# A hand-written order of instructions on TensorE, ScalarE and VectorE, re-ordered between a tenth and three eighths of the run

## The chip, the cores and the metric

The kernel runs on one core of one Trainium2 chip. The metric is the device time of one execution in microseconds (us). The profile gives beside it the span of one profiled execution and a row for every instruction. The engines are named as in the profile: PE is TensorE (matmuls), DVE is VectorE, ACT is ScalarE, POOL is GpSimd and SP is SyncE; the last two mostly issue DMAs here. A name such as L517 is line 517 of the kernel.

## The reference

Two stages. The first is an attention over a global and a local window, for 4 batches, 8 heads, 768 positions and 64 elements a head; the second is a feed-forward layer on the 3072 tokens that come out of it, with a squared relu between its two products.

```python
scores = scale * np.matmul(q, k.transpose(0, 1, 3, 2))
rel = pos[:, None] - pos[None, :]
is_global = pos[None, :] < 8
is_local = (rel >= 0) & (rel < 96)
scores = scores + bias                    # a slope per head times the distance
scores = np.where(is_global | is_local, scores, -1000000000.0)
a = softmax(scores);  attn_out = np.matmul(a, v)
x = attn_out.transpose(0, 2, 1, 3).reshape(3072, 512)
h = np.maximum(x @ w_in, 0.0)             # 512 to 2048
out = (h * h) @ w_out                     # 2048 to 512
```

## The kernel before, in words

**Tiling.** The 3072 tokens are cut into eight half-batches of 384 tokens, half 0 to half 7. Each goes through the same stages: its queries, keys and values are loaded by DMAs that GpSimd issues; queries and keys are turned (on TensorE for the first three halves, by DMA transposes that SP issues, `turn_by_dma`, from half 3 on); score jobs on TensorE (`score_unit`, L639, with 64 rows) fill two PSUM banks, ScalarE takes the exponential (L652), VectorE multiplies by a mask that holds the window and the slopes (`weigh`, L676); attention jobs multiply by the values (L700, or L1490 for the first two halves) and VectorE divides by the sums (`norm`: a reciprocal and a product, L708 and L710, or L1502 and L1504). The result is turned into `xt`, the transposed input of the feed-forward layer: by TensorE (`tile_to_x`, L1519) for halves 0 and 1, by SP's DMA transposes (L725) later.

**Layer 1.** For half 0, most of half 1 and a part of the others, plain jobs (`layer1`, L746) fill a PSUM bank with up to 512 columns; a relu on ScalarE (L773) or VectorE (L775) empties the bank, and a square on either (L787, L789) writes the hidden layer. The other groups of columns are computed with seven products in place of eight (L870), from weights that were added and subtracted beforehand (`in_mix`) and from sums of the tokens.

**Layer 2.** The first tile of tokens is plain (`layer2`, L1007). The others go in pairs of tiles with seven products (`layer2_pair`, L1093) from differences of quarters of w_out. These are made by `weight_sum` in `list_mix` (L517), in halves, c = 0 and c = 1. The first of these operations subtracts two parts of the same chunk of w_out, chunk c. w_out itself comes by four DMAs of a quarter each (`list_w_out`, L490), issued by GpSimd.

**What sets the order.** Every instruction group is an operation, listed once with what it needs. A string, `ORDER`, then says in which sequence they are emitted. A word has a letter for the engine (p TensorE, a ScalarE, d VectorE, g GpSimd, s SP, l a load on GpSimd's DMA queue) and a number: for p and l the number of the job in TensorE's or the loads' own list, for the others the number in one common list. So a124 and d124 are the same operation on two engines. Digits after a dot are the PSUM banks (0 to 7) that a TensorE job takes; a job without them goes on in a bank that it shares. An `@` names an SP operation that a load is to follow.

```python
for word in ORDER.split():
    ...
    op = lists.get(word[0], self.rest)[int(word[1:])]
    self.now, self.spare = [int(i) for i in banks], int(spare or 0) / 100
    op.result = op.emit("POOL" if word[0] == "l" else self.LETTERS[word[0]])
```

Each engine runs its own words strictly in their sequence and waits at a word whose data or whose buffer is not ready. The words of different engines do not order one another, except that data, PSUM banks and buffers pass in the order of emission. A job that takes a bank must wait until the operation that empties the bank's former holder is done.

Words that the prediction speaks of: d145 is the first half of the first weight difference (L517, c = 0), and l25 is the load of chunk 0 of w_out. d123 is the norm of attention job p55 (half 1). p49, p58 and p60 are plain layer-1 jobs of half 0, p56, p62, p63 and p65 of half 1, each over 512 columns of a bank (two groups of 128 hidden columns for 256 tokens, or four for 128 tokens). d131 is the relu of p60, d115 that of p49, and d122 and d129 are squares behind such relus. p72, p73, p74, p75 and p81 are plain layer-1 jobs of half 1 over 384 columns (one group for 384 tokens). p59 and p61 turn a piece of half 1's `xt` (L1519). p93 is an attention job of half 2, which needs the weighing d198. p106 and p107 are score jobs of half 3; p97, p100, p102, p104, p109 and p142 are products of layer 2 (L1093); p170 is an attention job of half 4. d221 is a norm of half 2, s222 the DMA transpose of its result, and s214 and s215 turn half 3's keys and queries.

Of the kernel before, what the change touches and what calls it, by code (L numbers as in the profile page):

```python
# [68 lines left out]
a138 d208 a209 d238 p91.5 a180 p92 d148 a142 s215 d217 p94.7 p102 d223 p95 d181 a243 d219 p96.2  # L69
d237 s218 p100.3 d236 p109 a216 d212 s224 d226 p104 d220 d241 l42 s227 d211 p107.57 d225 p108.23  # L70
d152 l41 p97 a253 s213 d256 a254 d139 l38@215 p99 a249 d143 d270 a250 l40@215 p111 a232 d188 l43
p112.23 d252 p106.57 p103.4 d190 a246 l39@215 a259 d244 p105 a260 l44 d251 d257 a247 p113.52
d255 s258 l45 p114.13 p116.0 s233 d228 a262 d248 p129.7 l46 a263 d230 p115.5 a266 d261 p120.2
a290 d229 p119.1 a271 d264 a267 d231 p123.7 d210 a269 d278 p122 s322 p125.3 d282 a281 p124 d239
a276 p121.5 d265 a291 p135.7 d283 s323 d279 a285 p117.6 a284 p130 a277 p127.1 d292 p128 p138
d321 a299 p140 a288 d268 p132.5 a305 a289 d272 s240 p126.7 a306 s280 p133 d286 p131.2 a308 p134
d296 p139.6 s273 d298 a297 l48@323 p141.7 a295 d307 p137 d324 s287 l54 d522 p136 a303 d393 p110
a301 l51 d309 a310 p118 d304 a300 l49@323 d293 p144.05 p145.63 d302 a328 l50 s294 p143.17 d311
a331 p142.2 d316 l47@323 a329 d317 a332 p146.0 l52 a274 d319 p147.6 a325 d431 l55 a320 a326
p149.53 d330 p148.41 l53 p150 d312 a336 d318 a337 d327 p157.7 a335 p155.4 a339 d334 p170.1 a350  # L80
d338 p151 a340 d368 a348 p158.0 a342 p167.5 s369 d313 p156.3 d351 p160 p159 d349 p152.1 a353
d314 p164.0 d395 a345 p162.3 s396 p161 d354 p154 d315 d356 p169.7 d357 a364 s397 p163 d341 p165
a358 p179.3 d360 a361 a359 d333 p168 p173 d343 a355 p175 d365 p172.4 d373 a376 p171.6 s245
p176.0 a381 d371 s275 s352 p174 d367 p178 d366 p153.3 a370 l56@397 d347 a377 s372 p166.4 d380
a374 a382 d398 l63 p177 p181 d378 a362 p180.7 l60 a346 p182 d383 a375 l57@397 p183.0 d379 s384
a387 a385 l61 a363 p186.14 d386 p185.63 p184.72 a403 p187.5 l71 d399 a407 a411 d400 l59 p188.6
a404 d414 d401 a408 l58@397 p189 a405 d394 a412 d410 p191.15 l62 d409 p192.73 a415 p190.24 a416
d413 p193 a420 d389 a417 p198.1 a418 d427 p204.2 a424 d435 p196.6 d390 p217.4 s436 d391 a432
d406 a425 p205.7 p202.1 d392 a445 s344 d487 p208 d441 a460 p200.3 a449 d426 a421 p197.4 d402
p209 a439 p211 d433 p195.1 p215.5 a430 d454 s434 p203.3 p216.4 d422 a442 d450 a443 p194 d478  # L90
s489 a459 d474 d458 p201.7 p213.2 d440 p221 s490 a456 p219 d423 a451 d419 p206 p207 d479 a446
p218 d481 a467 p220.4 d475 a444 p212 d465 p225.7 d429 s388 l68 p210.6 d455 s466 p199 d447 a462
l64 d491 a461 p214.4 d452 p222 a482 l67@490 p223 d457 a437 s453 a469 p228 d471 l70 d463 p224
s428 a494 d468 p229.36 l65@490 s488 a472 p234.04 d476 p231.15 a495 d470 p226.2 a501 l69 d480
d477 a496 p227.3 d492 l66@490 a507 d483 a502 d473 p239.1 l72 p233 a508 d503 a525 l73 d497
p235.62 a493 a464 p230.05 p232 d523 d484 a498 a448 p243.4 d504 p238.0 d506 s505 p245 a510 d513
p244.3 a531 p237 d486 a530 d485 a524 d514 p253 a499 p248 d518 p257.6 d542 s519 p247.5 d529
p241.7 p250 d534 a533 p236.4 d527 a538 d515 a511 s574 p251 a547 d500 p259.3 a517 p254 a549 d512
p255.7 s438 p268 d543 p261 d544 p242 a551 a563 d539 p246.2 a528 d509 p266.7 a532 p270 d559 a564
p265 p249.1 d558 p258.5 a540 s560 p260 d535 p267 d548 p256.7 a561 s545 p264 d546 a566 p240.5  # L100
a550 d536 s575 p252.6 d516 a526 p262 a576 p269 d552 p272 d565 d541 p263.0 p271 d577 p273 d567
a578 a553 d556 p277 d554 a562 d583 p279.1 s555 a594 a568 a557 p274.76 d569 p275.30 s537 p276.52
a584 p278 d598 a591 d599 a587 p280.7 d601 a602 a585 d596 p284 a592 d600 s597 a588 s572 p282.53
d586 p281.64 a603 p283.20 a607 d593 p287 a614 d666 a611 p289 a604 d617 d579 a605 d570 p286.5
a608 d620 s573 p288.2 d580 a618 p301.6 d589 s571 p304.4 d610 a637 p292 d606 a616 a641 d609
p321.3 a612 d669 d624 p303.0 p305 d640 p308 a642 p290.7 d582 d619 p293 a621 p319.0 d581 a626
d645 p294 d662 p310 a627 d613 p296 s663 p299 d648 p285.2 d630 p306.4 a615 s625 p295.0 d634 s595
p320 d643 p311.1 a664 p297.7 d590 a649 p312 d629 a646 p291.6 d650 p309.0 d622 p298 p314 a633
d647 p313 s623 a631 p316.6 d667 p300.0 a632 d670 p307 a665 d653 p318 p302 d651 a660 p324 d635
p322.1 d656 s636 a677 a661 d644 p323.5 d638 s657 d668 p315 a676 p317 a652 p333.0 d671 p341.6  # L110
p326 a705 a639 p332.7 d680 p325 a696 d675 d697 a654 p344.1 a658 d672 p347.4 a655 d710 p335.2
p349 a713 d699 p340 a659 p336.1 d681 p339.2 d678 a715 p353 d673 s679 a703 d700 p327.5 s628 d719
a704 d685 p338 d688 p357 d682 p346 d726 p343 p348.1 d712 a702 p337.4 d686 a714 p328 a701 a689
p345 d720 p352 p342 d708 p330 d674 a718 d706 a709 d683 p358 d711 p360 p329.2 d687 a731 d707 p355
d684 a692 p359 p351.4 a729 p364.6 d717 a690 a727 s691 d723 a693 p350.0 a728 d730 p331 a732 p356
d694 p354 d716 a695 p334 a724 d721 a725 d741 p363.3 d744 a722 p361 d745 d742 d698 p375.7 d737
# [1608 lines left out]
```

## Time and profile before

| | |
|---|---|
| median of three runs | 200.37 us (200.17 to 201.5) |
| the profiled execution's own time | 200.18 us |
| its span | 198.4 us |
| PE busy | 191.6 us, 2400 matmuls |
| DVE busy | 176.7 us, 448 instructions |
| ACT busy | 151.7 us, 321 instructions |
| POOL busy | 64.5 us, 80 instructions |
| granted TensorE clock | 1.0 |

The span runs from the first to the last instruction of the program in the profile; 1.8 us of the execution lie outside it. Busy time counts an engine's instructions and leaves waits out; PE's share of the span is therefore near one when it has few waits. Groups of the page have the line, the engine, what is written and read, the tile, the count, then busy time and mean, then the idle time ahead of them and what ended most of it. In the timeline a row has the start, the duration, the engine, the line and the operation; a bracket holds the idle time just before it and what ended it. In the chain of waits a row is a stretch of the chain that ended last.

### The profile page before, as it was taken

The numbers are of one execution on the slowest core, as the hardware profiler recorded it, in microseconds if no ns is written. First come the engines' busy times: TensorE is split into PE (matmuls) and PEld (weight loads), VectorE is DVE, ScalarE is ACT, GpSimd is POOL, SyncE is SP. The second block draws the span as 40 slices with busy tenths as digits, with TensorE's granted clock in tenths as the row PEclk, the third lists the DMA queues.
The fourth block names the chain that finished last, engine by engine and source line by source line (L and its number), as shares of the span: only waits on it lengthen the run. The fifth ranks groups of instructions, "written<-read, shape, count | busy, mean of one in ns | idle before, by whom it ended". The sixth has DMA issues, their size and how long they took to land.

```text
span 198.4 us, 6012 instructions
## 1 busy us (share of the span) xinstructions
PE 191.6 (97%) x2400; PEld 163.4 (82%) x2400; DVE 176.7 (89%) x448; ACT 151.7 (76%) x321; POOL 64.5 (32%) x80
## 2 busy tenths in 40 slices
PE   7998999999998999999999999999999999999993
PEld 3776899757997587789888998999889999999993
DVE  6778899899999989999989999899899996978971
ACT  6999997979444988966999679878897588769211
POOL 8985456637006902930392008600000000000000
DMA  5999999999997999999899599995531311201214
GB/s 154 189 185 201 194 171 180 207 184 155 175 182 73 178 181 227 114 132 133 228 128 151 93 218 134 167 182 128 96 101 37 115 36 40 107 2 56 106 53 159
DMA packets 102859, 27.52 MB, mean 139 GB/s; under 512 B 92976, under 2 KB 99888, under 8 KB 102832
## 3 DMA queue, kind: packets, MB, share of 16 engines
q0 software_dynamic: 70816, 13.11, 85.5%
q1 hardware_dynamic: 30816, 13.45, 30.1%
q10 hardware_dynamic: 1200, 0.59, 1.1%
q8 instruction: 18, 0.29, 0.6%
q14 instruction: 9, 0.07, 0.2%
HBM read 27.26 MB, written 6.29 MB: 169 GB/s over the span
## 4 chain that ended last, share of the span: by engine, by line
PE 69%; DMA 12%; DVE 9%; POOL 5%; issue 2%; SPq 1%; ACT 0%; POOLq 0%; DVEq 0%
PE yps L1093 27%; PE hps L870 19%; PE hps L746 13%; DMA v<-in_v_dram 7%; PE av L700 3%; DMA q<-sq 3%; PE sp L639 3%; DMA vb<-v 2%; PE yps L1007 2%; POOL sk L411 1%; POOL v L411 1%; POOL w_mix L422 1%; POOL sq L411 1%; DVE mixed L1058 1%; PE av L1490 1%
## 5 line engine op out<-in xcount | busy, mean ns | idle before, releaser
L652 ACT ACTIVATE ex<-sp 128x512 f16<-128x512 f32 x66 | 36.3, 632 | 5.7 <-PE sp L639 5.4
L1093 PEld LDWEIGHTS <-h 128*128 128x128 f16 x376 | 33.9, 98 | 4.3 <-DVE h L955 0.2
L746 PE MATMUL hps<-xt,w_in_sb 128*128 128x128 f16 (+2 forms) x288 | 35.7, 273 | 0.0
L255 ACT COPY kept<-hps 128x384 f32<-128x384 f32 x52 | 24.6, 490 | 12.2 <-PE hps L870 9.6
L930 DVE CUSTOM_DVE_ANT_0 hr<-hps,kept 128x384 f16<-128x384 f32 x58 | 30.4, 549 | 1.1 <-PE hps L870 0.6
L746 PEld LDWEIGHTS <-w_in_sb 128*128 128x128 f16 x288 | 23.5, 98 | 5.7
L1093 PEld LDWEIGHTS <-mixed 128*128 128x128 f16 x272 | 25.2, 98 | 3.6 <-DVE mixed L1058 0.2
L255 ACT COPY y<-yps 128x256 f32<-128x256 f32 (+2 forms) x39 | 14.8, 391 | 16.6 <-PE yps L1093 16.5
L411 POOL DMA_DIRECT2D sq<-in_q_dram x19 | 17.2, 906 | 31.3 <-DMA q<-sq 26.3
L411 POOL DMA_DIRECT2D sk<-in_k_dram x19 | 16.9, 893 | 26.1 <-DMA q<-sq 20.7
L870 PEld LDWEIGHTS <-w_in_sb 128*128 128x128 f16 x288 | 24.4, 98 | 0.9
L870 PEld LDWEIGHTS <-in_mix 128*128 128x128 f16 x272 | 22.8, 98 | 0.9
L870 PE MATMUL hps<-x_mix,in_mix 128*128 128x192 f16 x204 | 23.4, 246 | 0.0
L411 POOL DMA_DIRECT2D v<-in_v_dram x24 | 21.6, 911 | 2.9 <-DMA w_mix<-in_k_dram 1.5
L1093 PE MATMUL yps<-w_mix,h 128*128 128x256 f16 (+1 forms) x192 | 22.4, 264 | 0.0
L1093 PE MATMUL yps<-w_mix,mixed 128*128 128x256 f16 (+1 forms) x184 | 22.2, 268 | 0.0
L1093 PE MATMUL yps<-w_out_sb,h 128*128 128x256 f16 (+1 forms) x184 | 22.1, 268 | 0.1
L676 DVE TENSOR_TENSOR phat<-ex,mask 128x1024 f16<-128x1024 f16 (+1 forms) x36 | 20.7, 593 | 0.4 <-ACT ex L652 0.2
L953 ACT ACTIVATE h<-hr 128x768 f16<-128x768 f16 x25 | 20.9, 857 | 0.0
L870 PE MATMUL hps<-xt,w_in_sb 128*128 128x192 f16 x172 | 19.8, 246 | 0.0
L773 ACT ACTIVATE hr<-hps 128x384 f16<-128x384 f32 (+1 forms) x32 | 16.6, 555 | 0.8 <-PE hps L746 0.8
L787 ACT ACTIVATE h<-hr 128x768 f16<-128x768 f16 (+1 forms) x19 | 14.2, 771 | 1.1 <-DVE hr L775 1.1
(112 smaller groups left out, 353.3 us busy)
## 6 DMA issues: line engine op xcount, KB each, us to landing
out_dram<-y SPq DMA_DIRECT2D x23, 256.0 KB, 2.9
v<-in_v_dram POOLq DMA_DIRECT2D x24, 128.0 KB, 6.8
sq<-in_q_dram POOLq DMA_DIRECT2D x19, 128.0 KB, 6.2
sk<-in_k_dram POOLq DMA_DIRECT2D x19, 128.0 KB, 6.3
w_in_sb<-in_moe_w_in_dram POOLq DMA_DIRECT2D x4, 512.0 KB, 11.6
w_out_sb<-in_moe_w_out_dram POOLq DMA_DIRECT2D x4, 512.0 KB, 10.6
y<-in_k_dram ACTq DMA_DIRECT2D x2, 256.0 KB, 5.1
y<-in_q_dram SPq DMA_DIRECT2D x2, 256.0 KB, 4.5
```

What stands on the lines that cost most here:

```text
L255: nc.scalar.copy(out=out, in_=in_)
L411: dma = nc.gpsimd.dma_start(out=dst, in_=src[x.b, :, r0 + t * P:r0 + (t + 1) * P, :] .rearrange("h p d -> p h d"))
L639: nc.tensor.matmul(sp[h][:, i, :], lhsT=lhsT, rhs=queries(x, r % HT)[rows, a, :], start=True, stop=True)
L652: nc.scalar.activation(out=st["ex"][:, h], in_=sp[h], func=AF.Exp, scale=scale)
L676: eng(e).tensor_tensor(out=x.phat[a][:, :, t0:t0 + n], op=ALU.mult, in0=st["ex"][:, :, i0:i0 + 2 * n].rearrange("p e (t b) c -> p e t (b c ...
L746: nc.tensor.matmul(st["ps"][:, i * n:(i + 1) * n], lhsT=w_in_sb[:, kk, m * P:(m + 1) * P], rhs=x.xt[:, kk, c0:c1], start=kk == 0, stop=kk ...
L773: nc.scalar.activation(out=o, in_=i, func=AF.Relu)
L787: nc.scalar.activation(out=h2, in_=hr, func=AF.Square)
L870: nc.tensor.matmul(st[name][:, i * HC:(i + 1) * HC], lhsT=left(i, kk), rhs=right(kk), start=fresh and i == kk == 0, stop=kk == KK - 1, ski ...
L930: eng(e)._custom_dve(dve_ops.TENSOR_ADD_SAT, out=hidden(which)[:, :, cols], in0=sums(name), in1=st[kept], s0=3.4e38, s1=0.0)
L953: nc.scalar.activation(out=h2, in_=hr, func=AF.Square)
L1093: nc.tensor.matmul(st[bank_name][:, 0:n], lhsT=a(m), rhs=b(m)[:, cols], start=fresh and m == 0, stop=m == HK - 1, skip_group_check=not fresh)
```

## The change

Only the string `ORDER` differs. Each engine's operations are the same ones, and GpSimd's, SP's and the loads' words keep their sequence among themselves. The first part (to about 19 us, TensorE's first 35 jobs) keeps TensorE's sequence too. From there on 99 of TensorE's jobs, from p39 to about p136, stand at another place in its sequence; ScalarE's and VectorE's words are in another sequence as far as that, and 25 operations that VectorE did are done by ScalarE, 22 the other way round. From job p142 on the sequence of every engine is the old one. PSUM banks are dealt out anew all through the string. The core of the diff, the lines that hold the words named above:

```diff
--- before.py
+++ after.py
@@ -49,74 +49,74 @@
 KEEP = [0, 1, 2, 1, 6, 4, 3]
 
...
-d59 a61 p33.1 d67 p32.43 l17 a62 d83 p31.20 a23 p34.1 l21 p35.5 a79 d63 d84 a75 d89 l20 p39.4
-a76 d85 a80 l16 p38.12 a27 p37.05 p36.3 a99 l18 d64 a71 d81 p40.4 l25 a72 d87 a95 d82 p42.7 l26
-d73 p43.3 a90 d74 l27 a101 d105 p46.6 a91 d77 l28 d94 a96 p50.1 p45.0 l22 a100 p47.4 d78 d97
-a117 a86 d109 l23 p44.7 p41.5 a110 d108 p57.2 a102 d93 a112 d103 p48.1 p51.0 p49.6 a106 d88 d104
-a126 p53.7 p60.4 d98 a118 a115 d92 p55.5 a113 p52.3 d123 p54.2 a127 d111 a120 a114 d189 p61.0
-p58.6 a131 d119 p63.5 d121 p59.7 d203 p62.1 a122 d107 a130 d128 a133 p56.4 a134 d116 a129 d135
-p68.3 a132 p67.2 p70.7 a154 d199 p69.0 a157 d163 p81.6 d204 l32 a155 d124 p72.1 a164 a156 l24
-d165 p75.2 d160 a167 d158 a136 d161 p71.7 l29 d159 a172 d137 p87.41 a185 d205 p76.30 l33 p78.52
-d166 a173 p79.6 d187 a174 l31 p74.7 a196 d175 a179 p80.3 l30 d162 a197 d200 p82.0 d184 l34 d202
-p77.45 d145 l35 p86.13 p83 a193 d206 d147 a168 l36 p65.1 d182 a186 l37 d149 p84 a194 d150 a176
-p85 d198 a177 d125 p88.6 d146 a191 a183 d178 s192 p73.3 d153 a140 p89.4 a170 d141 a169 d201
-p93.5 a171 d207 p98.0 d195 p90 d234 d221 p101.1 d520 s222 d521 p64.7 a242 d235 d151 p66.3 s214
-a138 d208 a209 d238 p91.5 a180 p92 d148 a142 s215 d217 p94.7 p102 d223 p95 d181 a243 d219 p96.2
-d237 s218 p100.3 d236 p109 a216 d212 s224 d226 p104 d220 d241 l42 s227 d211 p107.57 d225 p108.23
...
+l21 p30.72 a61 d59 p33.1 d67 p32.43 a62 l20 d83 a23 p31.60 p34.5 a79 l16 d63 p35.1 a75 d84 d89
+l18 a27 p36.4 a80 d64 l25 a71 p39.5 d87 a76 l26 d82 p38.63 a72 p37.74 d94 l27 p40.0 a99 d81 l28
+a90 d88 p45.2 d85 a95 p46.5 l22 d73 a96 d109 p42.7 a110 l23 p57.1 d74 a91 d77 d105 p43.6 a100
+d78 a101 p41.3 d93 a111 p51.2 d97 p50.5 p44.4 d103 a86 p47.7 d104 a126 p53.0 p58.3 d117 d92 d108
+p54.1 a128 d98 d102 a118 p52.5 a106 p48.4 p60.3 d119 d120 d189 p59.2 p55.6 a130 p49.5 a112 d114
+d123 a127 p65.0 d145 a121 a113 p70.2 d131 p61.4 p69.7 d122 a133 p67.6 d129 p68.1 d115 a154 p75.3
+a163 l32 a132 p80.4 d164 d160 a157 l24 d107 p72.5 d155 a140 d149 p79.2 l29 a158 d187 a165 p81.6
+a182 l33 p71.0 a116 d203 d161 a172 l31 p82.1 d184 a185 d147 a162 l30 p56.2 a166 d199 d159 d156
+l34 p73.7 d167 a124 d141 p77.34 d169 l35 p86.60 a176 p87.52 d204 p83 a196 d146 l36 a177 d205
+p76.73 a193 d168 l37 p63.5 a183 d153 d200 p78.46 a197 p84 d151 a173 d178 a186 p88.2 d520 a179
+d198 p85 a194 d201 d206 p93.7 a191 p74.4 d221 a180 s192 p89.0 a207 d195 s222 a170 a174 d150
+p62.1 a136 d181 s214 p90 a171 d202 d175 a134 p94.7 p96.6 d212 s215 a208 d137 p91.4 a125 d211
+p66.3 d148 a135 d217 p92 a142 d223 a209 s218 p98.5 a216 d270 p64.1 d234 s224 d226 p95 d219 s227
+d152 p101.4 a220 a138 d225 d235 p97 l42 s213 a242 a238 d236 a143 p106.37 l41 p108.61 d188 p102
...
```

More of the change, by code (lines that the diff above doesn't have):

```diff
@@ L75 @@
[L75 to L92, printed above, removed]
@@ new lines @@
+d198 p85 a194 d201 d206 p93.7 a191 p74.4 d221 a180 s192 p89.0 a207 d195 s222 a170 a174 d150
+p62.1 a136 d181 s214 p90 a171 d202 d175 a134 p94.7 p96.6 d212 s215 a208 d137 p91.4 a125 d211
+p66.3 d148 a135 d217 p92 a142 d223 a209 s218 p98.5 a216 d270 p64.1 d234 s224 d226 p95 d219 s227
+d152 p101.4 a220 a138 d225 d235 p97 l42 s213 a242 a238 d236 a143 p106.37 l41 p108.61 d188 p102
+a253 l38@215 a246 d237 p99 a232 d243 l40@215 a247 d228 a254 p112.63 d248 p107.07 l43 a259 p104
+d230 a249 d229 l39@215 d231 a260 p120.1 d255 p116.6 a250 l44 d239 p109 a271 d244 a139 d190 l45
@@ new lines @@
+p113.03 p114.27 a262 p119.4 d261 l46 a278 d252 a266 p122 d276 p124 a267 p125.0 d256 p127.2 d521
+p129.4 d281 d210 p115.7 a290 d283 a285 p111 a263 d284 d268 p100.4 a288 a269 d264 a257 p130 d241
+s258 p133 d292 s233 p138 s322 p128 p123.3 d289 p121.7 d296 p140 s323 d282 a297 p134 d308 p126.5
+a291 p136 d277 p103.4 a305 d251 a309 s240 d298 p117.3 d265 a306 p139.6 d279 a324 p132.1 d272
+s280 p137 d286 a301 l48@323 p141.7 s273 d303 p105 l54 d522 a304 d321 p135.3 s287 l51 d393 p131.2
+a299 p110 l49@323 d293 a307 a295 p118 d302 a310 l50 s294 a300 d311 p144.50 l47@323 p145.36 a328
@@ new lines @@
+d316 p143.21 p142.7 a331 d317 l52 a329 d319 p146.5 a332 l55 d431 a274 p147.3 d330 l53 a325 a320
+d312 p149.06 a326 d318 p148.42 p150 a336 d327 a337 d334 p157.1 a335 d338 p155.4 a339 p170.5 a350
+p151 d368 a340 a348 p158.2 d313 s369 a342 p167.0 d351 p156.6 p160 d349 p159 s396 p152.5 d314
+a353 d395 p164.2 a345 p162.6 d354 p161 s397 p154 d315 d356 d357 p169.1 a364 p163 d341 p165 s245
+a358 d360 p179.6 s275 a361 s352 d333 a359 p168 p173 d343 a355 p175 d365 p172.4 d373 p171.3 a376
+p176.2 d371 a381 p174 d367 s372 p178 d366 p153.6 a370 l56@397 d347 a377 p166.4 d380 a374 a382
@@ new lines @@
+d398 l63 p177 p181 a362 d378 p180.1 l60 a346 p182 d383 a375 l57@397 p183.2 d379 s384 a387 a385
+l61 a363 p186.54 d386 p185.36 p184.17 a403 l71 p187.0 d399 a407 a411 d400 l59 p188.3 a404 d414
+d401 a408 l58@397 p189 a405 d394 a412 l62 p191.50 d410 p192.16 a415 d409 p190.74 a416 d413 p193
+a420 a417 d389 p198.5 a418 d427 a424 d435 p204.7 d390 p196.3 s436 d391 p217.4 d406 a432 a425
+p205.1 d392 s344 d487 p202.5 a445 p208 d441 a460 p200.6 a449 d426 a421 p197.4 d402 p209 a439
+p211 d433 p195.5 p215.0 a430 d454 p203.6 s434 p216.4 d422 a442 d450 a443 p194 d478 s489 a459
@@ new lines @@
+d474 d458 p201.1 p213.7 d440 p221 s490 a456 p219 d423 a451 p206 d419 p207 d479 a446 p218 d481
+a467 p220.4 s388 d475 a444 p212 d465 p225.1 d429 s466 p210.3 d455 p199 d447 a462 d491 a461
+p214.4 d452 p222 a482 l68 p223 d457 a437 s453 a469 p228 d471 l64 d463 p224 s428 a494 d468
+p229.63 a472 s488 l67@490 p234.24 d476 p231.50 a495 d470 p226.7 a501 l70 d480 d477 a496 p227.6
+d492 l65@490 a507 d483 a502 d473 p239.5 l69 p233 a508 d503 a525 d497 l66@490 p235.37 a493 a464
+p230.20 d523 p232 l72 d484 a498 a448 p243.4 d504 l73 p238.2 d506 s505 p245 a510 d513 p244.6 a531
@@ L122 @@
+a729 p364.3 d717 a690 a727 s691 d723 a693 p350.2 a728 d730 p331 a732 p356 d694 p354 d716 a695
+p334 a724 d721 a725 d741 p363.6 d744 a722 p361 d745 d742 d698 p375.1 d737 d733 p362 d738 s734
+d740 d739 p365.2 a735 d743 s736 p366 a747 d752 d756 d759 p369.5 d755 p371.4 a760 d748 p367 d753
+a763 d757 p372.7 d754 d767 d749 p374 d746 p373 d758 s750 p368 d766 a765 a764 p378 d751 p376 d771
+p377 d768 s772 p370 d769 s770 p379 a761 p380 s762 d773 s774 a775 a776"""
 class Op:
```

59 lines of the change are left out of this document (23 added, 36 removed).

## The prediction

> **What bounds the kernel now.** I read the page's busy times first, then a table of stretches around the part that is rewritten, then the places where TensorE really stands still, and last the landings of the loads. Page, busy time and DMA slices:
>
> ```profile
> PE 191.6 (97%) x2400; PEld 163.4 (82%) x2400; DVE 176.7 (89%) x448; ACT 151.7 (76%) x321; POOL 64.5 (32%) x80
> ...
> DMA  5999999999997999999899599995531311201214
> ```
>
> Busy time by stretches (per engine: us busy and instructions; last the mean DMA share times the stretch and GB/s):
>
> ```profile
> 18.00:36.00 18.00, 17.91 (x261) 16.23 (x259) 15.46 (x45) 16.70 (x37) 9.13 (x11) 1.00 1.76 185
> 36.00:52.00 16.00, 16.00 (x153) 10.71 (x150) 15.90 (x41) 12.90 (x27) 8.80 (x10) 1.00 1.87 183
> 52.00:60.00 8.00, 8.00 (x113) 7.41 (x110) 7.86 (x20) 4.16 (x8) 0.00 (x0) 1.00 1.23 160
> 60.00:75.00 15.00, 14.45 (x173) 10.79 (x171) 13.88 (x35) 11.80 (x26) 7.88 (x9) 1.00 1.57 149
> 75.00:87.00 12.00, 11.62 (x151) 8.83 (x149) 11.72 (x29) 10.75 (x24) 7.91 (x9) 1.00 1.61 161
> ```
>
> TensorE (third column of figures) is the bound: hardly a hole from 18 to 87. VectorE (fifth) has no slack from 36 to 60 (23.76 of 24 us), so nothing there can be late without being late for good. The DMA engines are nine tenths busy or more in every slice from 5 to 60 us. So a new order can win only the small holes of TensorE and can lose whatever it makes an engine wait. The holes, from the timeline of TensorE:
>
> ```profile
> 59.63 0.60 PE L1093 MATMUL yps<-w_out_sb,mixed 128*128 128x256 f16 x4
> ...
> 60.79 0.23 PE L639 MATMUL sp<-q,k 64*128 64x128 f16 x2 [0.55 <-DMA q<-sq]
> ...
> 80.74 0.22 PE L639 MATMUL sp<-q,kb 64*128 64x128 f16 x2
> 81.11 1.30 PE L1093 MATMUL yps<-w_out_sb,h 128*128 128x256 f16 x10
> ...
> 85.97 0.19 PE L700 MATMUL av<-v,phat 128*128 128x65 f16 x1
> 86.38 0.27 PE L700 MATMUL av<-v,phat 128*128 128x65 f16 x3 [0.23 <-DVE phat L676]
> ```
>
> p107 waits 0.55 for half 3's turned queries. p142 starts 0.15 after its forerunner's end (80.96). p170's second matmul, due some 0.03 after the first (three take 0.27 with 0.19 for one), comes at 86.38 in place of 86.00: 0.38. Together 1.08 us: that is all that can be won here.
>
> **The one move that meets a load.** Operations, DMAs and the order of SP's, POOL's and the loads' queues stay, so no transfer is issued past another one. I therefore asked of each operation that comes forward whether its data can be there. The one that stands out is d145, the first weight difference of layer 2 (L517), place 82 on VectorE before, place 61 after. It reads the first chunk of w_out, load l25:
>
> ```profile
> 27.88 0.75 POOL L490 DMA_DIRECT2D w_out_sb<-in_moe_w_out_dram  x1 [1.55 <-DMA w_in_sb<-in_moe_w_in_dram]
> ...
> L490 POOL DMA_DIRECT2D w_out_sb<-in_moe_w_out_dram x1: 754/754/754, 27.9 to 27.9; - x1
> ...
> DMA to landing us min/median/max: 8.3/8.3/8.3
> ...
> w_out_sb<-in_moe_w_out_dram POOLq DMA_DIRECT2D x4, 512.0 KB, 10.6
> ...
> 42.62 0.69 DVE L517 TENSOR_TENSOR w_mix<-w_out_sb 128x1024 f16<-128x1024 f16 x1
> ```
>
> Issued at 27.88, landed 8.3 later (the median of the four chunks is 10.6): 36.2. Now it runs at 42.62, 6 us after that. When does VectorE reach it in the new order? Right ahead of it is d123, the norm of attention job p55 of TensorE. Up to p55 the new order has run the jobs that the old has run up to p61, without p49 and p55 themselves, with p58 and p59 in addition.
>
> ```profile
> 31.12 0.28 PE L1519 MATMUL trx<-ident,tm 128*128 128x128 f16 x2
> ...
> 29.84 0.55 PE av L1490 x16
> ...
> 33.15 0.11 PE trx L1519 x2
> 33.26 1.75 PE hps L746 x16
> ...
> L1504 DVE TENSOR_TENSOR tm<-av,rec 128x256 f16<-128x256 f32 x12 | 5.1, 425 | 0.4
> ...
> L1502 DVE RECIPROCAL rec<-av 128x4 f32<-128x4 f32 x12 | 2.1, 174 | 0.4 <-PE av L1490 0.4
> ```
>
> (From the timeline, the chain of waits and the groups; the chain's lines, with a bare `x16`, are start, length, what.) p61 starts at 31.12. p49 and p58 are layer-1 jobs of 512 columns, 0.87 each (1.75 for two), and cancel; p55 (8 matmuls, half of 0.55) goes and p59 (0.11) comes: p55 starts near 31.0 and ends at 31.2; its norm takes 0.17 + 0.43. VectorE stands before d145 at 31.8 and waits **4.4 us**, to 36.2.
>
> Behind it stand d131, d122, d129, d115 and the copies of half 2's turned keys. d131 is the relu that empties PSUM bank 3 of p60; the next job on bank 3 is p75 (in the diff, p60.3 and p75.3). When does TensorE reach p75? Before it stand the jobs that stood before p81, except that p62, p63 and p56 have gone behind and p65 has come forward, four equal layer-1 jobs (0.87).
>
> ```profile
> 36.18 2.76 PE L746 MATMUL hps<-xt,w_in_sb 128*128 128x384 f16 x16
> ...
> 33.37 0.42 DVE L789 TENSOR_TENSOR h<-hr 128x512 f16<-128x512 f16 x1
> 33.70 0.68 DVE L775 TENSOR_SCALAR hr<-hps 128x512 f16<-128x512 f32 x1
> ...
> 36.34 2.60 PE hps L746 x16
> ```
>
> p81 starts at 36.18, so p75 is reached at 36.18 − 3 × 0.87 + 0.87 = 34.44. It may start when d145 (0.69 from 36.2, the next one overlaps its last 0.09, as 33.70 does the row of 33.37) and d131 (0.68, the relu of that shape) are done: 36.2 + 0.60 + 0.68 = 37.5. **TensorE loses 37.5 − 34.4 = 3.1 us.** Any earlier short wait only eats into these 3.1, since the end is set by the landing. Behind p75 the order just fits: two squares (0.42 less the overlap) and the relu d115 (bank 5, for p72) end at 37.4 + 2 × 0.33 + 0.68 = 38.7, and p72 is due after two jobs of 0.65 (2.60 for four) at 38.8.
>
> [...]
>
> **The other moves.** Terms beside the 3.1:
>
> - Half 3's scores. SP starts their two transposes behind the one that waits for norm d221:
>
> ```profile
> 51.29 0.56 DVE L710 TENSOR_TENSOR tm<-av,rec 128x384 f16<-128x384 f32 x1
> ...
> 51.94 1.28 SPq L725 DMA_TRANSPOSE xt<-tm  x1
> 53.33 1.43 SPq L596 DMA_TRANSPOSE k<-sk  x1
> 54.86 1.72 SPq L596 DMA_TRANSPOSE q<-sq  x1
> ...
> 54.86 5.79 DMA q<-sq
> ```
>
> From d145 to d221 are 34 VectorE operations in the new order; the old one ran 34 of the same kinds, d163 to d221, from 36.2 to 51.85 at 99% busy. So d221 ends at about 36.2 + 15.6 = 51.8, the queries land as now at 60.6. TensorE reaches p106, now the first to need them, after p97 more and p102, p104, p109, p100 less than p107 did (0.87 each): 60.23 − 2.6 + 3.1 = 60.7. The wait of 0.55 goes, for the late TensorE alone: −0.55.
> - Seven blocks of score jobs in place of six. A block costs about 0.1 (16 matmuls 0.55, 24 take 0.78, so 0.09 beside 0.23 for eight), and as much when the next kind starts: +0.2.
>
> ```profile
> 38.94 0.78 PE sp L639 x24
> ...
> 42.64 0.55 PE sp L639 x16
> ```
>
> - ScalarE and VectorE. 25 operations leave VectorE, 22 come to it, of 0.3 to 0.7 us: about 1.3 us less. It helps from 52 to 60, where ScalarE is busy 4.16 of 8 us, and it isn't enough to earn back the 4 us. With TensorE 2.5 us late at p142 and p170, their 0.15 and 0.38 go: −0.5.
> - New short waits. VectorE comes out of d145 late for a stage in which it had no slack. The first place that I find is p93:
>
> ```profile
> 47.47 0.33 PE L746 MATMUL hps<-xt,w_in_sb 128*128 128x384 f16 x1
> ```
>
> p73 starts at 47.47 now; before p93 the new order has run the same jobs, plus p73 and less p74 (both 0.65) and p62 (0.87), so p93 is due at 47.5 − 0.87 + 3.1 = 49.7. The weighing d198 that it needs is the 31st operation from d145, at 15.6/34 each done by 36.2 + 31 × 0.46 = 50.4, 0.7 late. The average is high for it, as the norm of d221 lies behind. Below: 0; a gain is excluded, TensorE's own work being fixed. Above: VectorE stays the bound up to p170, as it is now. Then its 4.4 less 1.3 come out whole (3.1), no hole is given back, and I allow it as much idle time again as it has now from 60 to 75 (15.00 − 13.88 = 1.1): +4.2 in all, 1.9 over the other terms. I take 0.4, between 0 and 0.7, since p93 is the only place where I find VectorE late.
>
> Sum: 3.1 − 0.55 + 0.2 − 0.5 + 0.4 = +2.6 on the profiled execution's 200.18: **202.8 us**. The median of the runs is 200.37, so the figure may come out 0.2 higher.
>
> Before p75 nothing decides: the swaps of 19 to 31 us end inside the 3.1. After p142 the order is the old one with banks renamed.
>
> **Rivals.**
>
> 1. *The load is there.* If l25 lands by 32, nothing waits at d145: the 1.08 us of holes mostly go, 0.2 for the block comes: 200.18 − 1.08 + 0.2 = 199.3. For it: the trace shows only one execution. Against: the DMA engines are nine tenths busy ahead of the landing, and the order of loads is untouched. It decides if the landing is 4 us earlier. 9%.
> 2. *VectorE becomes the bound* from p93 on: the upper end above, 200.18 + 4.2 = 204.4, from 203.7 up. For it: 99% from 36 to 52. Against: ScalarE takes work off. It decides if d198 and its like are over 0.7 late. 18%.
> 3. *TensorE slows after the wait.* The first eight matmuls of the run took 3.6 us, later ones of the same 512 columns 7.7/32 each:
>
> ```profile
> L323 PE MATMUL warm<-early 128*128 128x512 f16 x8 | 3.6, 631 | 1.2 <-DVE early L1576 1.2
> ...
> L1007 PE MATMUL yps<-w_out_sb,h 128*128 128x512 f16 x32 | 7.7, 380 | 0.0
> ```
>
> 0.45 against 0.24 each: near half rate for 3.6 us after standing idle. If 3.1 us idle brings that back, it costs half of 3.6: 204.6. The holes of up to 0.55 us in this trace brought no such thing. [...] 6%.
> 4. *The wait shows, and later slack gives back more*, a hole behind 87 us closing with it: 201 to 202. 9%.
>
> **How the numbers follow.** Forecast 54%, own range 201.8 to 203.8. 1% is 2.0 us, about what a measurement of this kernel can tell: slower begins at 202.4. Of the forecast's 54% some 36 lie above that; with rivals 2 and 3 that makes 0.60. The other 18, rival 1 (a gain of half a per cent) and rival 4 lie within 1%: 0.36. Faster needs a gain that the holes can't hold; for one that I haven't found stand the last 0.04. The range leaves out rival 1, that 0.04 and the outer parts of rivals 2 and 4, under 20% together: 201.0 to 204.7.
>
> **What would show it.** Right: the first L517 starts near 36.2 with a wait of about 4 us on the load of w_out_sb ahead of it; TensorE's longest wait is an L746 matmul starting near 37.5, released by an L775; no wait for q<-sq above 0.2; ScalarE's y of the first layer-2 tile later by 3. Wrong: L517 starts before 35, or TensorE crosses 34 to 38 without a hole; then the first rival holds. If the hole is there and the time isn't, the terms after p75 are mis-sized.

## The result and the profile after

The changed kernel takes 207.29 us (median of four runs, 206.38 to 207.85), the kernel before 200.75 beside it. The ratio is 1.0315, 95% interval 1.027 to 1.036: slower, by more than the forecast of 202.8, and outside its range of 201.0 to 204.7.

The page after, busy time of TensorE and the granted clock by slices of 5.2 us:

```profile
PE 193.7 (94%) x2400; PEld 164.0 (80%) x2400; DVE 176.1 (85%) x443; ACT 153.8 (75%) x326; POOL 64.5 (31%) x80
...
PEclk9999999699999999999999999999999999999998
```

One slice, around 39 us, ran at six tenths of the clock; the page of before has no such line, as its clock was full throughout. The stretches that the prediction showed, after (us of the stretch, busy us and instructions of TensorE, weight loads, VectorE, ScalarE and GpSimd, then the granted clock):

```profile
18.00:36.00 18.00, 16.73 (x246) 14.90 (x246) 12.90 (x41) 14.73 (x31) 9.96 (x12) 1.00 1.75 185
36.00:52.00 16.00, 14.40 (x121) 8.49 (x121) 14.72 (x37) 11.20 (x25) 7.95 (x10) 0.89 1.99 175
52.00:60.00 8.00, 8.00 (x111) 7.36 (x110) 7.86 (x21) 7.21 (x16) 0.00 (x0) 1.00 1.23 174
60.00:75.00 15.00, 12.88 (x146) 10.02 (x144) 11.70 (x26) 10.70 (x25) 7.88 (x9) 1.00 1.77 98
75.00:87.00 12.00, 12.00 (x137) 8.55 (x136) 11.47 (x29) 8.29 (x17) 3.48 (x4) 1.00 1.10 170
```

TensorE now stands idle in three of them: 1.27 + 1.60 + 2.12 = 4.99 us, against 1.02 before. From 36 to 52 the mean clock is 0.89; what that costs is worked out below. The last but one column, which the prediction called a share times the stretch, is the share itself; from 36 to 52 it is 1.99, so it isn't bounded by 1.

**The first wait.** VectorE's timeline, then TensorE's:

```profile
31.93 0.42 DVE L1504 TENSOR_TENSOR tm<-av,rec 128x256 f16<-128x256 f32 x1
36.26 0.69 DVE L517 TENSOR_TENSOR w_mix<-w_out_sb 128x1024 f16<-128x1024 f16 x1 [3.90 <-DMA w_out_sb<-in_moe_w_out_dram]
36.87 0.68 DVE L775 TENSOR_SCALAR hr<-hps 128x512 f16<-128x512 f32 x1
```

```profile
34.70 0.33 PE L578 MATMUL trp<-ident,sk 128*128 128x128 f16 x3
37.60 0.80 PE L746 MATMUL hps<-xt,w_in_sb 128*128 128x384 f16 x2 [2.57 <-DVE hr L775]
```

d145 waits 3.90 us for the load, and TensorE stands 2.57 us at p75 until d131 has emptied bank 3.

**The half clock.** TensorE alone in short stretches around that hole:

```profile
36.80:37.00 0.20, 0.00 (x0) 1.00 1.20 200
37.00:37.20 0.20, 0.00 (x0) 0.51 1.31 215
...
40.20:40.40 0.20, 0.20 (x2) 0.50 1.17 195
40.40:40.60 0.20, 0.20 (x3) 0.96 1.29 215
```

```profile
37.00:37.60 0.60, 0.00 (x0) 0.50 1.30 225
37.60:40.40 2.80, 2.80 (x9) 0.50 1.23 203
```

From 37.0 to 40.4, 3.4 us, the clock is at one half. TensorE is idle in the first 0.6 of it and works in the other 2.8, so the half clock costs 2.8 × 0.5 = 1.4 us here.

**A second wait, 30 us later.** VectorE, then TensorE:

```profile
67.24 0.36 DVE L847 TENSOR_TENSOR x_mix<-xt 128x384 f16<-128x384 f16 x1 [3.10 <-DMA xt<-tm]
```

```profile
67.66 0.51 PE L870 MATMUL hps<-x_mix,in_mix 128*128 128x192 f16 x4 [1.57 <-DVE x_mix L847]
...
70.12 0.23 PE L639 MATMUL sp<-q,k 64*128 64x128 f16 x2 [0.43 <-DVE y L257]
```

The first sum of half 2's tokens (d228) waits 3.10 us for the last DMA transpose of half 2's x (s227), and the layer-1 product p120, which reads that sum, 1.57. GpSimd's timeline and the chain of waits after:

```profile
60.77 1.75 POOL L411 DMA_DIRECT2D sq<-in_q_dram  x2 [11.67 <-DMA q<-sq]
...
60.91 6.24 DMA xt<-tm
```

The same two in the kernel before, GpSimd's timeline and the answer on the tile xt:

```profile
61.21 1.75 POOL L411 DMA_DIRECT2D sq<-in_q_dram  x2 [12.34 <-DMA q<-sq]
...
L725 SPq DMA_TRANSPOSE xt<-tm x1: 1206/1206/1206, 60.9 to 60.9; - x1
...
DMA to landing us min/median/max: 3.4/3.4/3.4
```

The transpose starts at 60.9 in both. Before, half 4's loads come 0.3 us behind it and it lands after 3.4 us; after, they come 0.14 ahead of it and it takes 6.2.

**The end of the profiled execution.** The final stores of y, after and before:

```profile
DMA to landing us min/median/max: 2.2/3.4/3.6
```

```profile
DMA to landing us min/median/max: 1.7/1.9/2.0
```

They add some 1.7 us to the profiled 207.85. From the start of the last matmul to the end of the span there are 5.0 us here, and 3.2 in the profile of every other kernel of this study, before included, so I leave this out. Whether the three runs without a profile (206.38 to 207.3) had it too can't be told. TensorE's last matmul starts at 201.14, against 195.18 before: 6.0 us later.

### The profile page after: what moved, and what is told of

The parts are those of the page before. It is cut to its first block, busy times and chain, and to the rows that moved or that the text cites. A ratio compares the mean times of both kernels' runs of the same rounds, so it can differ in the third digit from the quotient of the medians.

```text
span 206.1 us, 6004 instructions
## 1 busy us (share of the span) xinstructions
PE 193.7 (94%) x2400; PEld 164.0 (80%) x2400; DVE 176.1 (85%) x443; ACT 153.8 (75%) x326; POOL 64.5 (31%) x80
## 4 chain that ended last, share of the span: by engine, by line
PE 66%; DMA 16%; DVE 9%; POOL 5%; issue 2%; SPq 0%; ACT 0%; DVEq 0%; POOLq 0%
PE yps L1093 27%; PE hps L870 20%; PE hps L746 9%; DMA w_in_sb<-in_moe_w_in_dram 7%; DMA w_out_sb<-in_moe_w_out_dram 4%; PE av L700 4%; PE sp L639 4%; PE yps L1007 3%; DMA xt<-tm 3%; POOL v L411 2%; DVE phat L676 2%; DMA vb<-v 2%; POOL w_in_sb L483 1%; POOL w_mix L422 1%; DVE w_mix L517 1%
## 5 line engine op out<-in xcount | busy, mean ns | idle before, releaser
L746 PE MATMUL hps<-xt,w_in_sb 128*128 128x256 f16 (+2 forms) x288 | 37.4, 279 | 2.7 <-DVE hr L775 2.6
L255 ACT COPY kept<-hps 128x384 f32<-128x384 f32 x51 | 24.0, 488 | 12.9 <-PE hps L870 10.0
L411 POOL DMA_DIRECT2D sk<-in_k_dram x19 | 17.0, 896 | 31.8 <-DMA q<-sq 26.5
L255 ACT COPY y<-yps 128x256 f32<-128x256 f32 (+2 forms) x42 | 15.9, 391 | 13.5 <-PE yps L1093 13.3
L953 ACT ACTIVATE h<-hr 128x768 f16<-128x768 f16 x27 | 22.4, 853 | 0.8 <-DVE hr L938 0.8
L773 ACT ACTIVATE hr<-hps 128x384 f16<-128x384 f32 (+1 forms) x33 | 17.4, 547 | 6.2 <-PE hps L746 6.1
L787 ACT ACTIVATE h<-hr 128x512 f16<-128x512 f16 (+1 forms) x20 | 14.6, 743 | 2.0 <-DVE hr L775 2.0
```

Source lines behind the costliest of these rows:

```text
L255: nc.scalar.copy(out=out, in_=in_)
L411: dma = nc.gpsimd.dma_start(out=dst, in_=src[x.b, :, r0 + t * P:r0 + (t + 1) * P, :] .rearrange("h p d -> p h d"))
L746: nc.tensor.matmul(st["ps"][:, i * n:(i + 1) * n], lhsT=w_in_sb[:, kk, m * P:(m + 1) * P], rhs=x.xt[:, kk, c0:c1], start=kk == 0, stop=kk ...
L773: nc.scalar.activation(out=o, in_=i, func=AF.Relu)
L787: nc.scalar.activation(out=h2, in_=hr, func=AF.Square)
L953: nc.scalar.activation(out=h2, in_=hr, func=AF.Square)
```

## The experiments

The theory after the result: (1) d145, put ahead of the landing of its load, costs the wait at p75 and the half clock that follows it; (2) d228 and p120, put ahead of the last transpose of x, cost the second wait, and half 4's loads make it longer. The rival: the new order costs by itself, by its blocks and by its changes between ScalarE and VectorE, and the waits only collect that. Ratios are to runs of the kernel before on the same chip.

**d145 back behind the relus**

```diff
-d123 a127 p65.0 d145 a121 a113 p70.2 d131
+d123 a127 p65.0 a121 a113 p70.2 d131
...
-d155 a140 d149 p79.2
+d155 a140 d145 d149 p79.2
```

> The changed kernel with d145 alone moved back in VectorE's sequence, from behind d123 to ahead of d149, so that the relus and squares behind it (d131, d122, d129, d115) run before it. Theory (the wait for the load holds the relu of p60, TensorE stands for 2.6 us at p75 and then runs at half clock for some 3.4 us, which costs 1.4 more): VectorE doesn't wait at L517, TensorE crosses 34 to 41 us without a hole at clock 1.0, and the time falls by at least 4.0, from 207.3 to 203.3 or less; to 201 if the later wait at L847 goes with it. Rival (the new order as a whole, with its moves between ScalarE and VectorE, is what costs; the wait at d145 only collects a loss that would come anyway): the hole goes and the time stays above 205.

Measured: 205.04 us, ratio 1.0185 (1.013 to 1.024). The hole at p75 is gone and the clock is full from 34 to 41, but the time stops short of the theory's 203.3 and lies where the rival had it, just above 205. VectorE, then TensorE:

```profile
38.73 0.69 DVE L517 TENSOR_TENSOR w_mix<-w_out_sb 128x1024 f16<-128x1024 f16 x1 [1.29 <-DMA w_out_sb<-in_moe_w_out_dram]
```

```profile
66.97 0.50 PE L870 MATMUL hps<-x_mix,in_mix 128*128 128x192 f16 x4 [2.81 <-DVE x_mix L847]
```

The next weight difference, d149, now comes ahead of its own load, the next chunk; TensorE then waits 0.85 for a relu behind it (at 43.16). And the second wait has grown from 1.57 to 2.81: TensorE arrives earlier, while the transpose lands hardly sooner (VectorE goes on at 66.56 in place of 67.24).

**d145 with other data, its place untouched**

```diff
+                    a, b = (a[:, ms], b[:, ms]) if (i, ms.start) != (0, 0) else [
+                        w_in_sb[:, 0:4, n:n + HN] for n in (0, HN)]
-                    eng(e).tensor_tensor(out=t[i][:, ms], in0=a[:, ms], in1=b[:, ms],
-                                         op=ALU.subtract)
+                    eng(e).tensor_tensor(out=t[i][:, ms], in0=a, in1=b, op=ALU.subtract)
```

> The changed kernel with its order untouched, but d145 takes its difference from w_in, which landed long before, in place of the first chunk of w_out (the first half of the first weight difference is therefore not the one that the output needs). Theory (the wait is for the landing of that load and for nothing else): d145 runs at about 32.4 in place of 36.26, and the hole of TensorE and the half clock go as in the run with d145 moved back: 203.3 or less. Rival (d145 is late for another reason, such as its buffer or the place in the order): L517 still starts near 36 and the time stays at 207.

Measured: 204.29 us, ratio 1.0156 (1.009 to 1.022). VectorE's timeline (one line more in the file, so L517 is L519 here):

```profile
32.24 0.68 DVE L519 TENSOR_TENSOR w_mix<-w_in_sb 128x1024 f16<-128x1024 f16 x1
...
38.80 0.69 DVE L519 TENSOR_TENSOR w_mix<-w_out_sb 128x1024 f16<-128x1024 f16 x1 [1.93 <-DMA w_out_sb<-in_moe_w_out_dram]
```

d145 runs at 32.24, without a wait: it was the landing and nothing else. The theory's 203.3 isn't reached here either. Again d149 is next in line, until 38.8. Both runs together: (1) is true, but taking it away gives back 2 to 3 us of 6.5, for what stands behind is early too.

**d145 alone moved forward in the kernel before**

```diff
-a114 d189 p61.0 p58.6 a131 d119
+a114 d189 p61.0 p58.6 a131 d145 d119
...
-p77.45 d145 l35
+p77.45 l35
```

> The kernel before with d145 alone moved forward, to ahead of d119, where VectorE arrives at 31.9. Theory: VectorE waits 4.3 us for the load; d119, the norm that p59 needs, comes at 37.5 in place of 32.5, so TensorE stands from 33.0 to 37.5 and then runs at half clock for about 3 us: 4.5 + 1.5 less up to 1 us of later holes, 205 to 206. Rival (VectorE and TensorE have slack that takes up one late operation): within 1 us of 200.4.

Measured: 206.95 us, ratio 1.026 (1.019 to 1.034). One word out of some 1,200, put ahead of a landing, costs 2.6%, nearly as much as the whole change, though by a longer stop than there (4.46 us, not 2.57). The theory had 205 to 206. VectorE, TensorE, and TensorE's clock in stretches:

```profile
36.36 0.69 DVE L517 TENSOR_TENSOR w_mix<-w_out_sb 128x1024 f16<-128x1024 f16 x1 [4.40 <-DMA w_out_sb<-in_moe_w_out_dram]
```

```profile
37.67 0.40 PE L1519 MATMUL trx<-ident,tm 128*128 128x128 f16 x2 [4.46 <-DVE tm L1504]
```

```profile
35.20:35.40 0.20, 0.00 (x0) 0.57 1.19 200
35.40:42.00 6.60, 4.33 (x25) 0.50 1.24 208
42.00:42.20 0.20, 0.20 (x6) 0.86 1.16 195
```

Here the half clock lasts 6.8 us, twice the 3.4 and not the 3 that the theory took, and begins about 2 us after TensorE has gone idle (37.67 − 4.46 = 33.2).

**d145 moved forward only as far as the landing**

```diff
-d163 p81.6 d204 l32
+d163 p81.6 d145 d204 l32
...
-p77.45 d145 l35
+p77.45 l35
```

> The kernel before with d145 moved forward as in early_difference, but by less: ahead of d204, where VectorE arrives at 36.5, just after the landing of the load at 36.2. Theory (the place as such costs nothing, only its being ahead of the landing does): no wait at L517, the operations between move back by 0.6 us each, ratio 0.997 to 1.004. Rival (VectorE's order in this stretch is so tight that a weight difference among the copies of half 2's keys costs by itself): ratio 1.01 or more.

Measured: 200.73 us, ratio 0.998 (0.995 to 1.001).

```profile
36.71 0.68 DVE L517 TENSOR_TENSOR w_mix<-w_out_sb 128x1024 f16<-128x1024 f16 x1
```

No wait and no cost, at a place that VectorE reaches 4.8 us later. Between these two places lies the landing at 36.2, and the whole loss of 2.6%.

**Half 4's loads held behind the last transpose of x**

```diff
-p97 l42 s213
+p97 l42@227 s213
```

> The changed kernel, d145 where the change has it, with one more condition: the first load of half 4's queries (l42) is issued only behind the last DMA transpose of half 2's x (s227). Theory (that transpose, issued at 60.91, landed 6.2 us later because the load of the queries was issued at 60.77, just ahead of it; in the kernel before it was issued at 60.88 ahead of the load at 61.21 and took 3.4): the transpose lands near 64.3, VectorE's wait of 3.1 at L847 falls under 0.5, TensorE's wait of 1.57 at L870 goes, and the time falls by 1.5 to 2.2, to 205.1 to 205.8. Rival (the transpose is slow for other reasons): no change, 207.3.

Measured: 205.06 us, ratio 1.0166 (1.009 to 1.024), as the theory had it. VectorE, then GpSimd:

```profile
65.34 0.36 DVE L847 TENSOR_TENSOR x_mix<-xt 128x384 f16<-128x384 f16 x1 [1.04 <-DMA xt<-tm]
```

```profile
65.89 0.88 POOL L411 DMA_DIRECT2D sq<-in_q_dram  x1 [17.14 <-DMA xt<-tm]
```

The load waits for the landing, not only for the issue. The transpose lands 1.9 us sooner than in the changed kernel (VectorE goes on at 65.34 in place of 67.24), and TensorE doesn't wait at p120 any more. Not all of the 1.5% between 1.0315 and 1.0166 is the transpose: two of the four runs here kept a clock of 1.0, and none of the changed kernel's did. VectorE still waits 1.04, more than the 0.5 I expected: even alone the transpose lands about 1 us later than the 64.3 of the theory.

**TensorE kept busy during the first wait**

On top of held_loads, TensorE does 12 matmuls of zeros over 512 columns ahead of p68 (or, in the second kernel, 46 transposes of zeros).

```diff
-a133 p67.6 d129 p68.1 d115
+a133 p67.6 d129 p68.1+262 d115
...
-            state["ps"] = trp = bank([P, 2, HT, P], FP16, "trp")
-            warm(trp.rearrange("p i t c -> p (i t c)"))
+            if plan.spare: warm(bank([P, 512], FP32, "wps"))
+            plan.spare, state["ps"] = 0.0, bank([P, 2, HT, P], FP16, "trp"); trp = state["ps"]
```

(The transposes need the first of these edits alone.)

> The kernel with half 4's first load held behind the transpose (held_loads), and in addition twelve matmuls of zeros over 512 columns on TensorE ahead of p68, 2.56 us by the rate of the plain layer-2 matmuls, so that TensorE is busy while VectorE waits for the load. p75 still starts at 37.5. Theory (the half clock comes from the standing idle and costs 1.7 us of full clock): the granted clock stays 1.0 from 34 to 44 us, L746's 24 matmuls from p75 take about 4.0 us in place of 5.74, and the time falls by 1.4 to 1.8 from the 205.1 of held_loads. Rival (the half clock doesn't set the end; later waits swallow it): within 0.6 of 205.1.

> The same with 46 transposes of zeros in place of the matmuls, equally long (2.56 us). If the clock gate counts any work of TensorE: as with the matmuls, clock 1.0 and 203.3 to 203.7. If it doesn't count transposes as work: the clock halves within 34 to 40 us for 3.4 us as without filling, and the time stays near 205.1.

Measured: with matmuls 202.78 us, ratio 1.008 (1.004 to 1.012); with transposes 203.61, ratio 1.014 (1.008 to 1.020). TensorE's timeline and clock with matmuls:

```profile
34.49 2.75 PE L272 MATMUL wps<-early 128*128 128x512 f16 x12
...
37.64 4.06 PE L746 MATMUL hps<-xt,w_in_sb 128*128 128x384 f16 x24
```

```profile
37.60:41.50 3.90, 3.90 (x28) 1.00 1.23 204
```

And with transposes:

```profile
34.50 2.73 PE L275 MATMUL trp<-ident,early 128*128 128x128 f16 x46
...
37.57 4.06 PE L746 MATMUL hps<-xt,w_in_sb 128*128 128x384 f16 x24
```

```profile
37.60:41.50 3.90, 3.90 (x25) 1.00 1.24 205
```

The 24 matmuls take 4.06 us in place of the 5.74 of held_loads, on which both kernels build (5.43 in the changed kernel, where TensorE was idle in the first 0.6 us of the half clock), with p75 as late as ever. That is the price of the half clock: 1.7 us in held_loads' trace and 1.4 in the changed kernel's. The times go the same way, from 1.0166 to 1.008, which is 1.7 us, but they don't settle the size: the two intervals overlap, and two of held_loads' four runs had kept the clock without any filling. With the transposes the clock stayed full too: it was 1.0 in all four of their runs. That this kernel was 0.6% slower than the one with matmuls I can't explain by the clock; its profile has some small waits more behind 50 us (0.45 at 60.41 is one), and the intervals overlap.

**The early operations set back one after another**

```diff
-d155 a140 d149 p79.2
+d155 a140 d145 p79.2
...
-p82.1 d184 a185 d147 a162
+p82.1 d184 d149 a185 a162
...
-p73.7 d167 a124
+p73.7 d167 d147 a124
...
-p97 l42 s213
+p97 l42@227 s213
```

(and d145 gone from its place behind p65, as above.)

> The changed kernel with five words touched: d145 ahead of d149, d149 behind d184, d147 behind d167 (each weight difference behind the landing of its chunks of w_out, 36.2, 38.7 and 41.2), and half 4's first load held behind the last DMA transpose of half 2's x. Theory (these early operations are nearly all of the loss): VectorE waits under 0.5 us in sum at L517, L847's wait is under 0.6, and the time is within 1% of the kernel before, ratio 0.995 to 1.008. Rival (the new assignment to ScalarE and VectorE costs by itself): ratio 1.012 or more.

Measured: 203.16 us, ratio 1.0145 (1.008 to 1.021). The rival's number; the profile shows another wait all the same. VectorE, then TensorE:

```profile
45.95 0.61 DVE L257 COPY vb<-v 128x520 f16<-128x520 f16 x2 [1.30 <-DMA v<-in_v_dram]
```

```profile
48.16 0.20 PE L700 MATMUL av<-v,phat 128*128 128x65 f16 x1 [0.78 <-DVE phat L659]
49.09 0.26 PE L700 MATMUL av<-v,phat 128*128 128x65 f16 x3 [0.73 <-DVE phat L676]
```

The weight differences hardly wait any longer, and the next operation that is ahead of its load is d153, a copy of half 2's values. Two more kernels follow that trail.

```diff
-a183 d153 d200
+a183 d200
...
-d198 p85
+d198 d153 p85
```

> after_mended with one word more: d153, the copy of half 2's values that waited 1.30 us for its load (landed 45.95), behind d198, the weighing that p93 needs. Theory: TensorE's two waits at p93 (0.78 and 0.73) go, the time falls by 1.2 to 1.5 us, ratio 1.006 to 1.009. Rival (p93 needs d153 itself and the values land too late for the new place of p93): ratio stays at 1.0145.

Measured: 203.53 us, ratio 1.013 (1.009 to 1.017): not the 1.006 to 1.009 of the theory. TensorE's two waits shrink to 0.25 and 0.24, and VectorE comes to the next copy that is early:

```profile
54.24 0.30 DVE L257 COPY vb<-v 128x520 f16<-128x520 f16 x1 [1.99 <-DMA v<-in_v_dram]
```

```diff
-p96.6 d212 s215
+p96.6 s215
...
-d223 a209 s218 p98.5 a216 d270
+d223 d212 a209 s218 p98.5 d270
...
-a220 a138 d225
+a220 a138 a216 d225
```

> after_mended_2 with two words more: d212, a copy of half 3's values that made VectorE wait 1.98 us for its load (landed 54.2), behind d223; and a216, which made ScalarE wait 2.49 us for half 3's turned keys (landed 57.03), behind a138. Theory (what is left of the loss is again work in front of its own landing): TensorE's waits at p101 (0.57) and p97 (0.38) go, ratio 1.006 to 1.009. Rival (the rest is the order itself): ratio 1.011 or more.

Measured: 203.38 us, ratio 1.012 (1.008 to 1.017). A miss as well. TensorE's waits at p101 and p97 went, and these came:

```profile
59.76 0.23 PE L639 MATMUL sp<-q,kb 64*128 64x128 f16 x2 [0.67 <-ACT kb L255]
...
66.44 0.23 PE L639 MATMUL sp<-q,k 64*128 64x128 f16 x2 [0.43 <-DVE y L257]
```

Each repair moved the wait to the next transfer, or to the operation that I had moved out of its way (the copy kb is a216). So I found no variant of the new order as fast as the kernel before. In this last profile TensorE's closing row of 40 matmuls starts at 195.95, against 192.58 before, 3.4 us later. Of these, 1.6 are idle time of TensorE; its 2400 matmuls are also busy for 193.4 us in place of 191.6, and I have not taken that apart. How much of the last 1.2% is such waits and how much is the order by itself stays open.

**The kernel before, with its largest hole closed**

```diff
-p104 d220 d241 l42 s227 d211 p107.57 d225 p108.23 d152 l41 p97
+p104 d220 d241 l42 s227 d211 d225 p97 p107.57 p108.23 d152 l41
```

> The kernel before with one layer-2 product (p97) moved ahead of half 3's first score job (p107), and d225 emitted ahead of it with its place in VectorE's sequence unchanged. Theory (TensorE's wait of 0.55 for half 3's turned queries is the largest hole of the part that the change rewrites): p97 starts near 60.1, p107 at 61.0 without a wait, and the time falls by 0.4 to 0.7, ratio 0.997. Rival (the exponentials behind p107 are late by as much as p107 is): ratio 1.000.

Measured: 201.52 us, ratio 1.005 (1.002 to 1.009). p107 has its queries without a wait, and the kernel is half a per cent slower, not faster. VectorE, then TensorE:

```profile
75.31 0.61 DVE L257 COPY vb<-v 128x520 f16<-128x520 f16 x2 [1.99 <-DMA v<-in_v_dram]
```

```profile
76.58 0.20 PE L700 MATMUL av<-v,phat 128*128 128x65 f16 x1 [1.13 <-DVE phat L676]
```

All engines come to the stretch behind p107 half a microsecond earlier, and d321, a copy of half 4's values, comes ahead of its load and holds the weighing that TensorE needs. The second kernel sets d321 back as well:

```diff
-p128 p138 d321 a299
+p128 p138 a299
...
-a303 d393 p110
+a303 d321 d393 p110
```

> before_plus with one word more: d321, the copy of half 4's values that waited 1.99 us for its load (landed 75.3) and held d268, the weighing that TensorE then waited 1.13 us for, stands ahead of d393. Theory (closing the 0.55 us hole at p107 was worth its size, and d321, by then ahead of its landing, took it back): TensorE has no wait over 0.3 us from 50 to 80, ratio 0.996 to 0.999. Rival (the time is set elsewhere): 1.002 or more.

Measured: 200.81 us, ratio 1.001 (0.998 to 1.003). TensorE has no wait over 0.3 left between 50 and 80 us, its last matmul starts at 195.15 in place of 195.18, and the time is the same. The 0.55 us hole was worth nothing. From 60 to 75 TensorE has no idle time left, but from 75 to 87 it has 0.77 us in place of 0.38. Its longest wait there, 0.32 at 85.34, is for a sum of x that VectorE had to start late, behind the landing of a DMA transpose. That transfers which don't move with the order take back the whole gain is argued from this, not shown.

## Why the prediction was wrong

The mechanism was right up to p75, and two terms behind it were not: the clock, which the sum held at nothing, and the new short waits, which it had too small because it took the landings as fixed.

- **The wait for the load.** VectorE was to stand before d145 at 31.8, wait 4.4 us and go on at 36.2. It got there at 32.4, waited 3.90 and went on at 36.26. p75 was to start at 37.5: 37.60. Other data in the same place took the wait away. The load's landing held: d145 goes on between 36.10 and 36.36 in four traces in which it waited (the changed kernel, early_difference, held_loads and filled_matmuls). The weight differences that met the first, second and third chunk start at 36.26, 38.73 (late_difference) and, in after_mended_3, here:

```profile
41.28 0.69 DVE L517 TENSOR_TENSOR w_mix<-w_out_sb 128x1024 f16<-128x1024 f16 x1 [0.20 <-DMA w_out_sb<-in_moe_w_out_dram]
```

  In these traces one chunk of 512 KB lands every 2.5 us, and the first, issued at 27.9, came after 8.3 us again, as the prediction had read it from the trace of the kernel before. The first rival (the load is there) is refuted as to the landing. As to the time its 199.3 was wrong too: with the wait gone the new order took 204.3.
- **TensorE's loss of 3.1 us.** p75 was due at 34.44 and started at 37.60, 3.16 later. Only 2.57 of that is the wait at p75 itself: TensorE came there 0.6 late, at 35.03, since half 2's turns before it had waited for their data. The prediction had said that such waits only eat into the 3.1. Right in kind and size.
- **The clock: this term failed.** The sum held nothing for it; the third rival had it at 1.8 us and 204.6, with 6%. It measured 1.4 us here and 1.7 in held_loads. That its price came near is partly luck: it was taken from the eight matmuls at the start of the run, where the profile of the kernel before shows a granted clock of 1.00 (0 to 6 us), so that row doesn't show a half clock. The step that failed is the reading that a stop of 3.1 us costs no more than itself: I took holes of up to 0.55 without effect as evidence against, though nothing in that trace lay between 0.55 and 3.1. Here 2.57 was followed by 3.4 us at half clock, and 4.46 in early_difference by 6.8. When the half clock began, TensorE had stood idle for 2.0 us in the changed kernel and in early_difference; in held_loads it had been idle for 2.51 and at work again for 0.8. What sets the start and the length no run here shows.
- **New short waits, 0.4 within 0 to 0.7: this term failed too.** It measured 1.57 + 0.43 = 2.0. I looked for an operation that VectorE brings too late (d198 for p93, where TensorE then didn't wait) and took the new places of p120 and d228 for harmless. The question that found d145, whether the data can be there, points at them too, but with the old landing of s227, 64.3 (60.88 + 3.4), it gives little: VectorE stood before d228 at 64.14, so the wait would have been 0.2, and TensorE, which came to p120 at 66.1, would not have waited. What failed is the sentence that no transfer is issued past another one. Each queue kept its order of issue, but the two queues didn't keep theirs against each other: half 4's loads, which wait for half 3's turned queries, came 0.4 us sooner (60.77 in place of 61.21) and so ahead of s227 (60.91), and its landing moved by 2.8 us (6.2 after its start, in place of 3.4). With the loads held behind it, the wait at p120 was gone.
- **The holes that go** (0.55 at p107, 0.15 and 0.38 later) went as forecast. 3.1 − 0.55 + 0.2 − 0.5 + 0.4 was the sum. With the measured 3.16, 2.0 and 1.4 in their places it is 3.16 − 0.55 + 0.2 − 0.5 + 2.0 + 1.4 = 5.7, of the 6.0 by which the last matmul came later; the other 0.3 I haven't followed up, and the 0.2 and the 0.5 were not measured one by one. The kernel in which the clock and the second wait are repaired (filled_matmuls) takes 202.78, where 202.8 was forecast for all but these two. That the two agree to the decimal is luck: against the kernel before beside it, it is 0.8% slower (0.4 to 1.2), where the forecast is 1.3%.
- **VectorE as the bound** (second rival) didn't come: 11.70 us of 15 busy from 60 to 75. Its "not enough slack" was a wait for transfers each time.

## What to carry to other kernels

In a stage in which the loads land one after another, as the chunks of w_out do here every 2.5 us, ask of every operation that an order brings forward, not of the most conspicuous one alone, when its data lands; an engine that runs its words in sequence pays for one early operation with all that stands behind it (d145 alone, ahead of its landing, cost 2.6%). Then price the stop itself: to the wait belongs the half clock that can follow it (1.4 and 1.7 us here), and the transfers that change places because the issuers were released at other moments (s227 took 6.2 us in place of 3.4). An order kept within each queue is not an order kept between queues, as half 4's loads and s227 showed. And a hole that is closed upstream of landings that stay where they are may be worth nothing, as the 0.55 us here.

## What the runs showed of the hardware that was not expected

- Stops of TensorE of 2.57 us (the changed kernel) and 2.51 us (held_loads) went with 3.4 us at half clock; one of 2.81 us did not. In the changed kernel the mean clock of the four runs was 0.987 to 0.991. In late_difference the stop of 2.81 us left it at 1.0 in the profiled run, and one of the four runs had 0.989. In held_loads two of four runs kept 1.0, and the profiled one, with a stop of 2.51 us, had 0.989:

```profile
37.45 5.74 PE L746 MATMUL hps<-xt,w_in_sb 128*128 128x384 f16 x24 [2.51 <-DVE hr L775]
```

  The start of the stretch at half clock was not tied to the start of the stop in these two traces: it came 2.0 us after TensorE went idle in the changed kernel (35.03, 37.0) and 0.8 us after it had started again in held_loads (38.3).
- Transposes on TensorE seem to hold the clock like matmuls: with 46 of them in the stop it was 1.0 in all four runs, as it was 0.999 to 1.0 in the ten runs with matmuls. As two of held_loads' four runs kept 1.0 with the stop left empty, this is a strong hint and no proof.
- The order of issue of two DMAs from different engines, some tenths of a us apart, went with the time that a DMA transpose took. In the changed kernel half 4's loads come 0.14 us ahead of s227 and it took 6.2 us; in the kernel before they come 0.3 us behind it and it took 3.4. held_loads shows that taking the loads away from it helps (VectorE, which waits for its landing, goes on at 65.34 in place of 67.24); that a change of order by these tenths is enough is argued from the two traces, and not shown.
